# First batch entry: where the weight loads queue, how the coarse queries and keys are made, and unread products between the blocks

## The chip, the cores and the metric

One core of a Trainium2 chip runs the whole program. The time is that of the device in microseconds (us); three runs of the kernel before gave 1096.65, 1097.37 and 1098.7, median 1097.37.

## What is computed

Three layers follow each other. Attention takes 2 batch entries, 8 heads, 576 positions and 64 dimensions; each head is computed twice and added: once coarse, on means of four neighbouring positions, and once fine, where a position sees only positions less than 4 away.

```
q_d, k_d, v_d = means of 4 neighbouring positions of q, k, v        # 144 positions
out_d     = softmax(q_d k_d^T / 8) v_d,  each row repeated 4 times
out_local = softmax(q k^T / 8 where |i - j| < 4) v
x         = out_d + out_local                                       # 1152 x 512
```

Then come a mixture of 8 experts (512 to 1024 and back, weighted by a table P that 8 rounds of normalising rows and columns make) and an MLP (512 to 2048 and back). All inputs are float32.

## The kernel before, in words

Attention is done by units: a unit is a pair of heads of one batch entry. There are four units per entry, eight in all, and a unit is four blocks: the coarse block "c" and the fine blocks 0, 1, 2 of three tiles of 64 queries each. The loop over `stream` (from line 741) goes through the 32 blocks. For each it traces `scores` of this block, `turn` (the transpose of the softmax) of the block two back and `values` of the block three back. In the last two blocks of a unit it traces `setup` of the next unit, in three groups (g = 0, 1, 2), and in the last block `load` of the unit after that.

`load` (291) issues a unit's q, k and v on SyncE's queue. The q and k tile has one buffer, so the next load waits until `setup` has read it. `setup` (313) transposes three tiles of q and k on TensorE into a bank of PSUM (322). VectorE sums four neighbours from that bank (327) into `qkd`, and scales the queries out of it into `flat`, a tile whose other halves are zero (333). ScalarE and VectorE copy keys and queries for the fine blocks (337 to 339). GpSimd sums v (346, 347).

`scores` (349) multiplies: for the coarse block `flat` with `qkd` (355), for a fine block first the additive mask through an identity (362, bf16) and then queries with keys (368). VectorE takes the maximum (375), ScalarE the exponential (379), VectorE the division (380 to 382).

The weights of the experts are split into two parts of lower precision. `fetch_first` (113) loads one piece of the first weights by SyncE's queue into `raw` (two buffers), ScalarE rounds it (132, 138), VectorE and GpSimd make sums and remainders (133, 111, 139). `fetch_second` (141) does the same for the second weights (151 to 154). The first three pieces are traced in the attention loop, at line 747: one fetch in the second block of each of units 1 to 6.

From the third step after the middle of the stream on, `beside` (714) adds the first expert's products (601, 660) between the blocks of the second batch entry, a given number of columns for each block.

The order on each engine within attention is made by a planner: it plays the program through with its own costs and puts, on each engine, the instruction traced first among those that its play holds ready. After attention the order of TensorE is written out by hand. Each engine then runs its list strictly in that order.

Banks of PSUM: scores of the first batch entry take m0, m1 and m2 in turn (68); transposes take four banks called "at"; values take "y". In the second entry all of these take "at", and m0 to m2 belong to the expert's products (592).

Of the kernel before, what the change touches and what calls it, by code (L numbers as in the profile page):

```python
# [9 lines left out]
F32 = mybir.dt.float32  # L10
# [4 lines left out]
ALU = mybir.AluOpType  # L15
AX = mybir.AxisListType
# [4 lines left out]
def attention_moe_mlp(ctx: ExitStack, tc: tile.TileContext, q, k, v, w_gate, w1, w2, w_in, w_out, out):  # L21
    nc = tc.nc
    B, H, S, D = q.shape
    NT, DM = out.shape
    E, _, FF = w1.shape
    F2 = w_out.shape[0]
    P = 128
    R = 4
    SD = S // R
    HC = SD // 2  # L30
    QT = 64
    NQ = S // QT
    NB = 3
    CT = SD // NB
    KW = QT + 2 * R
# [15 lines left out]
    SUMS = 4  # L51
    OPS = 7

    const = ctx.enter_context(tc.tile_pool(name="const", bufs=1))
    xp = ctx.enter_context(tc.tile_pool(name="xp", bufs=1))
    wp = ctx.enter_context(tc.tile_pool(name="wp", bufs=3))
# [7 lines left out]

    def bank(tag, name):
        if tag == "m":
            tag = f"m{next(turns) % 3}"
        return ps.tile([P, 512], F32, tag=tag, bufs=4 if tag == "at" else 1, name=name)

    turns = count()  # L70
# [30 lines left out]
    s_out = scratch("s_out", [F2 // (2 * P), 2, P, 2, DM])  # L101

    weights = {}

    def weight_sums(sums, w):

# [168 lines left out]
    for x in fine + flat:  # L275
        nc.gpsimd.memset(x, 0.0)

    class Unit:


# [10 lines left out]
        def load(self, first=False):  # L291
            b, h0 = self.b, 2 * self.u
            self.qk = qk = ap.tile([P, NQ, 2, D], F32, tag="qk", bufs=1, name="qk")
            cuts = [slice(NB * g, NB * g + NB) for g in range(NB)] if first else [slice(0, NQ)]
            for cut in cuts:
                for w, src in enumerate((q, k)):
                    for hh in range(2):
                        nc.sync.dma_start(
                            qk[w * QT : (w + 1) * QT, cut, hh],
                            src[b, h0 + hh].rearrange("(t p) d -> p t d", p=QT)[:, cut],  # L300
                        )
            self.vw = vw = ap.tile([KW, NQ, 2, D], F32, tag="vw", name="vw")
            for t, w0 in ((0, 0), (NQ - 1, S - KW)):
                nc.sync.dma_start(vw[:, t], v[b, h0 : h0 + 2, w0 : w0 + KW, :].rearrange("h p d -> p h d"))
            for hh in range(2):
                src = v[b, h0 + hh, QT - R :, :]
                windows = bass.AP(tensor=src.tensor, offset=src.offset, ap=[[D, KW], [QT * D, NQ - 2], [1, D]])
                nc.sync.dma_start(vw[:, 1 : NQ - 1, hh], windows)
            self.vd = vd = ap.tile([HC, 2, 2, R, D], F32, tag="vd", bufs=1, name="vd")
            for hh in range(2):  # L310
                nc.sync.dma_start(vd[:, :, hh], v[b, h0 + hh].rearrange("(c p r) d -> p c r d", c=2, r=R))

        def setup(self, g):

            if g == 0:
                self.kT = ap.tile([P, NQ, QT], F32, tag="kT", name="kT")
                self.qkd = ap.tile([P, NQ, 2, QT // R], F32, tag="qkd", name="qkd")
            qkd = self.qkd
            tb = self.bank("tb", 1)
            tiles = slice(NB * g, NB * g + NB)  # L320
            for j in range(NB):
                nc.tensor.transpose(
                    tb[:, j * P : (j + 1) * P], self.qk[:, NB * g + j].rearrange("p h d -> p (h d)"), ident
                )
            tb = tb[:, : NB * P]
            tbv = tb.rearrange("x (t w p) -> x t w p", t=NB, w=2)
            nc.vector.tensor_reduce(
                qkd[:, tiles].rearrange("x t w g -> x (t w) g"),
                tb.rearrange("x (t g r) -> x t g r", g=QT // R, r=R), axis=AX.X, op=ALU.add,
            )  # L330
            for hh in range(2):
                half = slice(hh * D, (hh + 1) * D)
                nc.vector.tensor_scalar(
                    self.flat[half, g, hh].rearrange("x (j g) -> x j g", j=NB), qkd[half, tiles, 0],
                    SCALE / (R * R), None, op0=ALU.mult,
                )
            nc.scalar.mul(self.kT[:, tiles], tbv[:, :, 1], SCALE)
            nc.vector.tensor_copy(fine[g][:D, :, 0], tbv[:D, :, 0])
            nc.scalar.copy(fine[g][D:, :, 1], tbv[D:, :, 0])
            if g:  # L340
                return
            vd = self.vd

            self.vs = vs = ap.tile([HC, 2, 2, D], F32, tag="vs", name="vs")
            for c in range(2):
                nc.gpsimd.tensor_tensor(vd[:, c, :, 0:2, :], vd[:, c, :, 0:2, :], vd[:, c, :, 2:4, :], op=ALU.add)
                nc.gpsimd.tensor_tensor(vs[:, c], vd[:, c, :, 0, :], vd[:, c, :, 1, :], op=ALU.add)

        def scores(self, blk):

            sc = self.bank("sc", 0)
            if blk == "c":
                rows, w = 2 * CT, SD
                for i in range(NB):
                    nc.tensor.matmul(
                        sc[:rows, i * w : (i + 1) * w], self.flat[:, i].rearrange("x h q -> x (h q)"),
                        self.qkd[:, :, 1], start=True, stop=True,
                    )
            else:
                rows, w = P, KW  # L360
                tiles = range(NB * blk, NB * blk + NB)
                nc.tensor.matmul(
                    sc[:, : NB * w], identb, mask[:, blk : blk + NB].rearrange("p t w -> p (t w)"),
                    start=True, stop=False,
                )
                for i, t in enumerate(tiles):
                    w0 = min(max(t * QT - R, 0), S - KW)
                    nc.tensor.matmul(
                        sc[:, i * w : (i + 1) * w], fine[blk][:, i].rearrange("x h q -> x (h q)"),
                        self.kT.rearrange("x t q -> x (t q)")[:, w0 : w0 + KW], start=False, stop=(i == NB - 1),  # L370
                    )
# [369 lines left out]
    for n in range(len(stream) + LAG + 1):  # L741
        if n < len(stream):
            x, blk = stream[n]
            i, j = divmod(n, len(blocks))
            x.scores(blk)
            if j == 1 and 1 <= i <= 6:
                (fetch_first if i % 2 else fetch_second)((i - 1) // 2, (i - 1) // 2)
            if j >= 2 and i + 1 < len(units):
                for g in ((0, 1), (2,))[j - 2]:
                    units[i + 1].setup(g)  # L750
                if j == 3 and i + 2 < len(units):
                    units[i + 2].load()
        for lag, what in ((LAG, "turn"), (LAG + 1, "values")):
            if 0 <= n - lag < len(stream):
                x, blk = stream[n - lag]
                getattr(x, what)(blk)
        while columns < (n - begin) * DENSE:
            columns += next(side, 1 << 30)
# [100 lines left out]
```

## Time and profile before

| | |
|---|---|
| runs | 1096.65, 1097.37, 1098.7 us |
| profiled execution, first to last instruction (its span) | 1094.7 us |
| TensorE busy | 1060.0 us, 97% |
| VectorE busy | 727.0 us, 66% |
| ScalarE busy | 555.2 us, 51% |
| GpSimd busy | 537.6 us, 49% |

No other time of the profiled execution is shown than its span; the median of the runs is 2.67 us above it. A busy share is an average over the whole span; the first batch entry takes about the first 70 us of it. In the rows below, PE is TensorE, PEld its weight loads, DVE VectorE, ACT ScalarE, POOL GpSimd and SP SyncE. A number in brackets behind a timeline's row is the idle time of the engine just before, with what ended it. In a timeline several instructions of one kind are merged into one row with their count.

### The profile page before, as it was taken

What the parts mean: (1) busy time and instruction counts of PE and PEld (TensorE: products, weight loads), DVE (VectorE), ACT (ScalarE), POOL (GpSimd) and SP (SyncE); (2) the same over time, 40 slices, a digit from 0 to 9 for tenths busy, and PEclk for the clock granted to TensorE, in tenths of its full rate; (3) what the DMA queues carried; (4) which work ended last, traced back from release to release, by engine and by line L of the source; (5) the groups of instructions that cost most, each with busy time, mean ns of one, the idle gap of its engine ahead of it and who ended that gap; (6) DMA issues with size and microseconds to landing.
All of it is one profiled execution on the core that took longest, in us unless ns stands there. A gap on an engine that the chain in (4) does not pass through costs nothing.

```text
span 1094.7 us, 17873 instructions
## 1 busy us (share of the span) xinstructions
PE 1060.0 (97%) x6385; PEld 938.0 (86%) x6385; DVE 727.0 (66%) x1532; ACT 555.2 (51%) x1443; POOL 537.6 (49%) x569
## 2 busy tenths in 40 slices
PE   6899999999999999999999999999999998999998
PEld 5678888998987889888888988898898897889987
DVE  6889665565666676667657665766663578766765
ACT  4667645343444444434444443444443567676763
POOL 6735235464467676756766455354664212222321
PEclk9579999999999999999999999999999999999999
DMA  8454101111235334434443332223333273244112
GB/s 175 118 115 109 49 27 55 62 58 40 84 100 145 115 110 143 132 105 127 122 134 102 117 112 93 100 93 110 102 116 116 106 278 139 113 175 182 68 39 87
DMA packets 133497, 119.70 MB, mean 109 GB/s; under 512 B 35744, under 2 KB 111776, under 8 KB 133408
## 3 DMA queue, kind: packets, MB, share of 16 engines
q1 hardware_dynamic: 133408, 118.56, 35.0%
q8 instruction: 50, 0.82, 0.3%
q14 instruction: 39, 0.32, 0.1%
HBM read 93.11 MB, written 25.43 MB: 108 GB/s over the span
## 4 chain that ended last, share of the span: by engine, by line
PE 40%; POOL 5%; DMA 5%; DVE 3%; issue 2%; ACT 2%; SPq 0%; POOLq 0%; ACTq 0%; DVEq 0%
PE yps L660 21%; PE m L601 19%; DMA raw<-in_moe_w_out 2%; POOL sums L111 2%; POOL w2l L154 1%; POOL cva L188 1%; POOL cva L197 1%; DMA raw<-in_moe_w 1%; DMA raw<-in_moe_w_in 1%; DVE cva L178 1%; POOL w1l L139 1%; DVE cva L189 0%; DVE cva L179 0%; DVE cva L182 0%; DMA s_out<-cva 0%
## 5 line engine op out<-in xcount | busy, mean ns | idle before, releaser
L601 PE MATMUL m<-xh,w1h 128*128 128x320 f32 (+1 forms) x1120 | 336.6, 301 | 13.1 <-ACT t L610 6.3
L601 PE MATMUL m<-xh,w1l 128*128 128x320 f32 (+1 forms) x1120 | 332.5, 297 | 0.0
L601 PE MATMUL m<-xl,w1h 128*128 128x320 f32 (+1 forms) x1120 | 332.4, 297 | 0.0
L601 PEld LDWEIGHTS m<-xh,w1h 128*128 128x128 f32 x1120 | 212.2, 189 | 38.7 <-ACT t L610 10.8
L601 PEld LDWEIGHTS m<-xl,w1h 128*128 128x128 f32 x1120 | 212.4, 190 | 11.8
L601 PEld LDWEIGHTS m<-xh,w1l 128*128 128x128 f32 x1120 | 212.2, 190 | 0.2 <-issue 0.2
L660 PE MATMUL yps<-w2h,hh 128*128 128x512 f32 x502 | 198.5, 395 | 0.0
L660 PE MATMUL yps<-w2l,hh 128*128 128x512 f32 x502 | 198.4, 395 | 0.0
L660 PE MATMUL yps<-w2h,hl 128*128 128x512 f32 x502 | 195.5, 389 | 0.0
L660 PE MATMUL yps<-w2h,h 128*128 128x512 f32 x436 | 153.3, 393 | 0.0
L615 DVE TENSOR_TENSOR c<-m,t 128x256 f32<-128x256 f32 (+1 forms) x160 | 72.3, 452 | 100.9 <-PE m L601 99.5
L139 POOL TENSOR_TENSOR w1l<-sums,w1h 128x512 fp32r<-128x512 f32 x72 | 95.8, 1345 | 78.2 <-ACT w1h L138 54.4
L571 POOL TENSOR_TENSOR ab<-ab,up 128x320 f32<-128x320 f32 (+1 forms) x64 | 53.9, 843 | 157.2 <-ACT ln L567 109.8
L154 POOL TENSOR_TENSOR w2l<-raw,w2h 128x512 fp32r<-128x512 f32 x72 | 94.9, 1339 | 71.4 <-ACT w2h L153 71.3
L558 ACT ACTIVATE hh<-c 128x256 fp32r<-128x256 f32 (+1 forms) x138 | 60.0, 443 | 125.0 <-DVE c L615 123.3
L559 DVE SCALAR_TENSOR_TENSOR hl<-c,hh 128x256 fp32r<-128x256 f32 (+1 forms) x138 | 91.4, 668 | 35.0 <-ACT hh L558 33.2
L660 PEld LDWEIGHTS yps<-w2h,hl 128*128 128x128 f32 x502 | 94.4, 188 | 21.3
L677 DVE SCALAR_TENSOR_TENSOR acc<-yps,pr,acc 128x512 f32<-128x512 f32 x117 | 86.9, 743 | 29.5 <-PE yps L660 29.4
L660 PEld LDWEIGHTS yps<-w2h,hh 128*128 128x128 f32 x502 | 94.7, 189 | 12.6 <-DVE acc L673 0.2
L660 PEld LDWEIGHTS yps<-w2l,hh 128*128 128x128 f32 x502 | 94.7, 189 | 11.1 <-issue 0.4
L660 PEld LDWEIGHTS yps<-w2h,h 128*128 128x128 f32 x436 | 82.6, 189 | 14.8
L188 POOL TENSOR_TENSOR cva<-cva,raw 128x512 uint32<-128x512 uint32 x32 | 42.7, 1336 | 95.2 <-DVE raw L185 76.6
(134 smaller groups left out, 1700.7 us busy)
## 6 DMA issues: line engine op xcount, KB each, us to landing
raw<-in_moe_w SPq DMA_DIRECT2D x72, 256.0 KB
raw<-in_moe_w SPq DMA_DIRECT2D x36, 512.0 KB
w1h<-s_in SPq DMA_DIRECT2D x10, 896.0 KB
w1l<-s_in SPq DMA_DIRECT2D x10, 896.0 KB
raw<-in_moe_w_in SPq DMA_DIRECT2D x32, 256.0 KB
raw<-in_moe_w_out SPq DMA_DIRECT2D x16, 512.0 KB
w2l<-s_out SPq DMA_DIRECT2D x10, 512.0 KB
w2h<-s_out SPq DMA_DIRECT2D x10, 512.0 KB
```

Of the source, the lines that this page charges most:

```text
L111: nc.gpsimd.tensor_tensor(sums[i], a, b, op=op)
L139: nc.gpsimd.tensor_tensor(lo[:, part], sums, hi[:, part].bitcast(F32), op=ALU.subtract)
L154: nc.gpsimd.tensor_tensor(lo[:, i], raw[:, i], hi[:, i].bitcast(F32), op=ALU.subtract)
L178: nc.vector.tensor_scalar(a, high, 0x07FFFFFF, 3, op0=ALU.bitwise_and, op1=ALU.logical_shift_left)
L188: nc.gpsimd.tensor_tensor(a, a, low, op=ALU.add)
L558: nc.scalar.activation(hh, c, AF.Relu)
L559: nc.vector.scalar_tensor_tensor(out=hl, in0=c, scalar=0.0, in1=hh.bitcast(F32), op0=ALU.max, op1=ALU.subtract)
L571: nc.gpsimd.tensor_tensor(ab, ab, up, op=ALU.subtract)
L601: nc.tensor.matmul(b[:, :h], x[:, i, kk, :], y[s][:, i, kk, :], start=(not more and n == 0), stop=(n == 5), skip_group_check=more,)
L615: nc.vector.tensor_tensor(c, b[:, :h], t, op=ALU.add)
L660: nc.tensor.matmul(y, a[:, f, tok], b[:, f, :], start=(start and m == 0), stop=(stop and m == 5))
L677: nc.vector.scalar_tensor_tensor(out=acc[t], in0=y, scalar=pr[:, t, e : e + 1], in1=acc[t], op0=ALU.mult, op1=ALU.add,)
```

## The change

Four things change, all within attention.

1. The coarse queries and keys of the first batch entry come from TensorE. A small constant `coarse` holds, for each head of the pair, the matrix that adds four neighbours (queries scaled, the other head's columns zero). For each group of `setup`, six products of 48 columns with q and k as the weights go into a bank `pool` of the "at" kind; after the third group one copy by VectorE brings the bank into `parts`, from which the coarse scores read. The sums (327) and the scalings (333) are left out for these four units; the second entry keeps them.
2. Products of the mask with the identity, 360 columns in bf16, which nobody reads: 14 ahead of everything else, 3 after the scores of each block of the first entry. They are ordered behind the product traced before them; those between blocks have a lower priority.
3. These products write bank m2, so the scores of the first entry take m0 and m1 in turn.
4. The three pieces of weights that line 747 fetched one by one are traced with the loads of units 3, 4, 5 and 6, and their loads stand behind the last load of that unit on SyncE's queue.

```diff
+    START, BETWEEN, LOW = 14, 3, -60
-            tag = f"m{next(turns) % 3}"
+            tag = f"m{next(turns) % 2}"
+    BEHIND = {3: [(0, 0)], 4: [(0, 1), (1, 0)], 5: [(1, 1), (2, 0)], 6: [(2, 1)]}
+    group = ap.tile([P, 2, QT // R], F32, tag="qkd", name="group")
+    nc.vector.tensor_reduce(
+        group.rearrange("p w g -> p (w g)"), ident.rearrange("p (g r) -> p g r", r=R), axis=AX.X, op=ALU.add
+    )
+    coarse = ap.tile([P, 2, 3, QT // R], F32, bufs=1, name="coarse")
+    nc.vector.memset(coarse, 0.0)
+    for hh in range(2):
+        nc.vector.tensor_scalar(coarse[:, hh, hh], group[:, 0], SCALE / (R * R), None, op0=ALU.mult)
+        nc.vector.tensor_copy(coarse[:, hh, 2], group[:, 1])
+    warm = mask.rearrange("p t w -> p (t w)")
+    idle = ps.tile([P, 512], F32, tag="m2", name="idle")
+    def keep_warm(n):
+        for _ in range(n):
+            tc.keep_in_program_order(nc.tensor.matmul(idle[:, : (NB + 2) * KW], identb, warm, start=True, stop=True))
+    keep_warm(START)
...
+            if self.b == 0:
+                pool = self.pool[:, : NB * 3 * CT]
+                spread = pool.rearrange("x (i s j g) -> x i j s g", i=NB, s=3, j=NB)
+                for j in range(NB):
+                    for hh in range(2):
+                        nc.tensor.matmul(
+                            spread[hh * D : (hh + 1) * D, g, j], self.qk[:, NB * g + j, hh],
+                            coarse[:, hh].rearrange("p s g -> p (s g)"), start=True, stop=True,
+                        )
+                if g == NB - 1:
+                    self.parts = ap.tile([P, NB, 3 * CT], F32, tag="qkd", name="parts")
+                    nc.vector.tensor_copy(self.parts.rearrange("x i c -> x (i c)"), pool)
...
+            if self.b:
+                nc.vector.tensor_reduce(
...
+                    if self.b == 0:
+                        q_, k_ = self.parts[:, i, : 2 * CT], self.parts[:, :, 2 * CT :]
...
-            if j == 1 and 1 <= i <= 6:
-                (fetch_first if i % 2 else fetch_second)((i - 1) // 2, (i - 1) // 2)
+            if x.b == 0:
+                with tc.high_priority(offset=LOW):
+                    keep_warm(BETWEEN)
...
                     units[i + 2].load()
+                    with tc.issue_after(units[i + 2].loaded.ins):
+                        for f, second_part in BEHIND.get(i + 2, ()):
+                            (fetch_second if second_part else fetch_first)(f, f)
```

## Rows read from the trace of the kernel before

**Rows 1.** The page: busy time of TensorE over the span, and its clock by slices

```profile
PE 1060.0 (97%) x6385; PEld 938.0 (86%) x6385; DVE 727.0 (66%) x1532; ACT 555.2 (51%) x1443; POOL 537.6 (49%) x569
...
PEclk9579999999999999999999999999999999999999
```

**Rows 2.** The page: the chain that ended last, by engine

```profile
PE 40%; POOL 5%; DMA 5%; DVE 3%; issue 2%; ACT 2%; SPq 0%; POOLq 0%; ACTq 0%; DVEq 0%
```

**Rows 3.** Stretches: us long, busy of PE, PEld, DVE, ACT, POOL, clock, DMA share, GB/s

```profile
6.60:26.00 19.40, 16.50 (x78) 14.02 (x79) 16.26 (x42) 11.71 (x47) 10.95 (x16) 1.00 0.86 188
26.00:33.00 7.00, 4.72 (x61) 3.74 (x60) 6.83 (x18) 5.87 (x27) 7.00 (x10) 0.95 0.57 157
33.00:66.00 33.00, 29.71 (x174) 23.62 (x174) 28.79 (x75) 20.26 (x81) 21.13 (x25) 0.50 0.62 129
...
78.00:88.00 10.00, 9.33 (x63) 7.86 (x63) 8.88 (x30) 5.67 (x23) 2.56 (x4) 0.66 0.38 84
...
140.00:1094.70 954.70, 938.26 (x5461) 835.02 (x5459) 618.01 (x1220) 464.31 (x1088) 466.47 (x471) 1.00 0.33 108
```

**Rows 4.** Timeline of TensorE: start us, us, line, what, count

```profile
8.56 0.57 PE L362 MATMUL sc<-mask,identb 128*128 128x216 bf16 x2
...
14.45 1.54 PE L322 MATMUL tb<-ident,qk 128*128 128x128 f32 x6 [0.27 <-DMA qk<-in_k]
15.78 0.39 PE L362 MATMUL sc<-mask,identb 128*128 128x216 bf16 x1
...
27.41 0.57 PE L424 MATMUL pv<-et,vw 72*64 72x64 f32 x12
...
28.19 0.82 PE L322 MATMUL tb<-ident,qk 128*128 128x128 f32 x6
...
46.62 1.49 PE L322 MATMUL tb<-ident,qk 128*128 128x128 f32 x6
...
50.39 0.91 PE L424 MATMUL pv<-et,vw 72*64 72x64 f32 x12
...
66.70 0.36 PE L601 MATMUL m<-xh,w1h 128*128 128x256 f32 x1
```

**Rows 5.** VectorE by line and shape, 0 to 66 us: busy us, mean ns

```profile
L327 DVE TENSOR_REDUCE qkd<-tb 128x96 f32<-128x384 f32 x13 | 7.1, 549 | 6.2 <-PE tb L322 6.2
...
L333 DVE TENSOR_SCALAR flat<-qkd 64x48 f32<-64x48 f32 x24 | 4.6, 193 | 0.3
...
L375 DVE TENSOR_REDUCE small<-sc 96x3 f32<-96x432 f32 x4 | 2.4, 597 | 2.3 <-PE sc L355 2.3
```

**Rows 6.** VectorE by line and shape, 100 to 160 us: a plain copy

```profile
L671 DVE COPY acc<-yps 128x512 f32<-128x512 f32 x2 | 1.4, 689 | 0.0
```

**Rows 7.** Timeline of VectorE: the same product late and on time

```profile
33.54 3.70 DVE L382 TENSOR_TENSOR ex<-ex,small 128x216 f32<-128x216 f32 x1
...
39.53 0.37 DVE L382 TENSOR_TENSOR ex<-ex,small 128x216 f32<-128x216 f32 x1
```

**Rows 8.** Timeline of GpSimd: mask, first weight product, the one beside Rows 7

```profile
6.20 0.97 POOL L267 TENSOR_SCALAR_AFFINE_SELECT mask<-mask 64x216 bf16<-64x216 bf16 x3
...
26.62 2.64 POOL L139 TENSOR_TENSOR w1l<-sums,w1h 128x512 fp32r<-128x512 f32 x2
...
33.83 2.48 POOL L154 TENSOR_TENSOR w2l<-raw,w2h 128x512 fp32r<-128x512 f32 x2
```

**Rows 9.** Timeline of SyncE's queue: first weight load; last loads of units 3, 4

```profile
13.57 0.94 SPq L124 DMA_DIRECT2D raw<-in_moe_w  x2
...
38.14 0.59 SPq L311 DMA_DIRECT2D vd<-in_v  x1
...
61.70 0.77 SPq L311 DMA_DIRECT2D vd<-in_v  x2
```

**Rows 10.** Timeline of TensorE: its first products, and its wait at 33 us

```profile
6.61 2.15 PE L322 MATMUL tb<-ident,qk 128*128 128x128 f32 x9 [6.61 <-POOL mask L267]
...
33.34 1.18 PE L393 MATMUL tp<-ident,ex 96*72 96x96 f32 x6 [2.18 <-DVE ex L382]
```

More of the change, by code (lines that the diff above doesn't have):

```diff
@@ L310, in load @@
             for hh in range(2):
-                nc.sync.dma_start(vd[:, :, hh], v[b, h0 + hh].rearrange("(c p r) d -> p c r d", c=2, r=R))
+                self.loaded = nc.sync.dma_start(
+                    vd[:, :, hh], v[b, h0 + hh].rearrange("(c p r) d -> p c r d", c=2, r=R)
+                )
         def setup(self, g):
@@ L316, in setup @@
                 self.kT = ap.tile([P, NQ, QT], F32, tag="kT", name="kT")
-                self.qkd = ap.tile([P, NQ, 2, QT // R], F32, tag="qkd", name="qkd")
-            qkd = self.qkd
+                if self.b:
+                    self.qkd = ap.tile([P, 3 * NQ, QT // R], F32, tag="qkd", name="qkd")[:, : 2 * NQ]
+                    self.qkd = self.qkd.rearrange("x (t w) g -> x t w g", w=2)
+                if self.b == 0:
+                    self.pool = self.bank("pool", 1)
             tb = self.bank("tb", 1)
@@ L324, in setup @@
                 )
+            if self.b == 0:
[6 more added lines that the diff above has]
+                            coarse[:, hh].rearrange("p s g -> p (s g)"), start=True, stop=True,
+                        )
+                if g == NB - 1:
+                    self.parts = ap.tile([P, NB, 3 * CT], F32, tag="qkd", name="parts")
+                    nc.vector.tensor_copy(self.parts.rearrange("x i c -> x (i c)"), pool)
             tb = tb[:, : NB * P]
             tbv = tb.rearrange("x (t w p) -> x t w p", t=NB, w=2)
[L327 to L335, printed above, removed]
-                )
+            if self.b:
+                nc.vector.tensor_reduce(
+                    self.qkd[:, tiles].rearrange("x t w g -> x (t w) g"),
+                    tb.rearrange("x (t g r) -> x t g r", g=QT // R, r=R), axis=AX.X, op=ALU.add,
+                )
+                for hh in range(2):
+                    half = slice(hh * D, (hh + 1) * D)
+                    nc.vector.tensor_scalar(
+                        self.flat[half, g, hh].rearrange("x (j g) -> x j g", j=NB), self.qkd[half, tiles, 0],
+                        SCALE / (R * R), None, op0=ALU.mult,
+                    )
             nc.scalar.mul(self.kT[:, tiles], tbv[:, :, 1], SCALE)
@@ L354, in scores @@
                 for i in range(NB):
[L355 to L358, printed above, removed]
+                    if self.b == 0:
+                        q_, k_ = self.parts[:, i, : 2 * CT], self.parts[:, :, 2 * CT :]
+                    else:
+                        q_, k_ = self.flat[:, i].rearrange("x h q -> x (h q)"), self.qkd[:, :, 1]
+                    nc.tensor.matmul(sc[:rows, i * w : (i + 1) * w], q_, k_, start=True, stop=True)
             else:
```

## The prediction

> **What bounds the kernel now.** I read the page first. TensorE is busy for 1060.0 of 1094.7 us [rows 1], and in the chain that ended last it has by far the largest part that belongs to one engine [rows 2]. That is an average over stages, so I cut the span. From 140 us to the end TensorE is busy for 938.26 of 954.70 us [rows 3]: 16.4 us are idle there, the order of TensorE is written out by hand, and the change touches nothing of it. What the change can win lies ahead of 140 us, and there mostly in the first batch entry, up to about 66 us: at 66.70 the first product of the experts runs [rows 4]. A stage that ends earlier lets everything behind it start earlier, since TensorE is the bound of that rest.
>
> Within 6.6 to 66 us two engines are nearly full: TensorE is busy for 16.50 + 4.72 + 29.71 = 50.9 of 59.4 us and VectorE for 16.26 + 6.83 + 28.79 = 51.9 [rows 3]. The granted clock says 0.50 for 33 to 66 us, the lower level of 1.2 GHz, although TensorE was busy for 29.71 of those 33.00 us. The clock's row also says 1.00 for the first 26 us, and this the reader should not believe: six transposes of the same shape take 1.54 us at 14.45, 0.82 at 28.19 and 1.49 at 46.62 [rows 4]. The last stands in the stretch with 0.50, so the first ran at the lower level too, and the view does not show it. So 16.50 + 29.71 = 46.2 us of TensorE's work ran at the lower level. The full level costs 0.82/1.49 = 0.55 of that for the transposes and 0.57/0.91 = 0.63 for twelve products of the values [rows 4]; I take 0.59.
>
> **Part 1, coarse sums on TensorE.** Removed from VectorE, for four units of three groups: 12 sums of 0.549 and 24 scalings of 0.193 [rows 5], 6.6 + 4.6 = 11.2 us. Added there: four copies of 128x432 out of a bank. No row has that copy; a maximum over 432 columns takes 0.597 [rows 5], a copy of 512 columns 0.689 [rows 6]. I take 0.58 by columns from the second, 0.55 to 0.69 as ends: 2.3 us. The preparation of `coarse` is six small instructions in the first 6.6 us, where VectorE has next to nothing to do, so it costs nothing. VectorE's net is -8.9 us (ends -9.0 and -8.4). TensorE gets 18 products of 48 columns per unit, 72 in all. The nearest row is the product of the values with 64 columns: 0.57/12 = 0.048 us at the full level and 0.91/12 = 0.076 at the lower [rows 4], so 3.4 to 5.5 us. The coarse scores themselves keep their shape. The q and k buffer is released six short products later, 0.3 us at most per group, ahead of a load that is not late; cost 0.
>
> **Part 2, unread products.** A product of 216 bf16 columns takes 0.39 alone, two in a row 0.57 [rows 4], so each further one 0.18, at the lower level. For 360 columns that is 0.30, and 0.17 at the full level (by 0.55). The 48 between blocks are then 8.2 us at the full level and 14.4 at the lower. They are meant for idle time of TensorE; at the lower level there are only 59.4 - 50.9 = 8.5 us of it.
>
> The 14 at the start need the whole mask, which GpSimd ends at 6.20 + 0.97 = 7.17 [rows 8]. If they stand ahead of the first transposes, now at 6.61 [rows 10], they end at 7.17 + 14 x 0.30 = 11.4, and the transposes start 4.8 us late. If the planner puts them behind the transposes, the delay is less, down to 0. The price shrinks again: what stands between the first transposes and those of unit 1 (6.61 to 14.45, where a load is waited for) is 7.8 us at the lower level and 7.8 x 0.59 = 4.6 at the full one, so unit 1 would begin at 16.0 instead of 14.45. I take +1.6 us, ends 0 and +4.8.
>
> What is bought is the clock. If it stays at the full level, TensorE's work in the stage is 46.2 x 0.59 + 4.72 = 32.0, with the additions of both parts (3.4, 8.2, and 14 x 0.17 = 2.4) 46.0 us. VectorE's is 51.9 - 8.9 = 43.0.
>
> **Part 3, two banks for scores instead of three.** TensorE may run two blocks ahead of the softmax rather than three. There are 16 blocks in 59.4 us, 3.7 us each, and two banks allow 7.4 us from a bank's first product to its last exponential. No row shows a wait for such a bank. I take 0; the upper end is one short wait of 0.3 us in each block, 4.8 us.
>
> **Part 4, weight loads.** The first one now goes out at 13.57, ahead of the loads of unit 2, and its last remainder ends at 26.62 + 2.64 = 29.26 [rows 8, 9], 15.7 us later. In the change it stands behind unit 3's last load, now at 38.14 [rows 9], so it would be ready at 38.7 + 15.7 = 54.4, for a first use at 66.70. If loads come 5 us earlier and the first use 10, 7 us of slack are left. The next two stand behind unit 4's loads, now at 61.70 [rows 9]. The same instructions run on all engines, only later, so I take 0 for the work. What the early conversions did can be seen: a product of VectorE that takes 0.37 us at 39.53 took 3.70 at 33.54 [rows 7], while GpSimd made two remainders of the second weights from 33.83 to 36.31 [rows 8]. So the move clears units 0 to 2 of this and brings it to units 3 to 5. Ends: -3.3 (this one stall goes for good) and +3.3 (one more).
>
> A rule of the Trainium skill speaks against counting more here ("SBUF — State Buffer", section "Who interferes with whom"): a VectorE instruction with two operands from SBUF and a GpSimd one that reads SBUF exclude each other, and the later is blocked for the whole of the other. By it each remainder on GpSimd can block VectorE wherever it is put, so the move would win 0; by the one row at 33.54 alone it would win 3.3. The rows agree in part: the product is listed 0.29 us ahead of GpSimd's two remainders, yet it ended 0.93 us behind them.
>
> **The sum.** With the clock up, 46.0 us of TensorE and 43.0 of VectorE share a stage that today holds 51.9 of the fuller engine in 59.4, a fill of 0.87. At that fill VectorE's 43.0 need 49.4 us, and TensorE's 46.0 still fit in it (0.93, and 8.2 of them are filler). The stage is 10.0 us shorter; less 1.6 for the start is -8.4 us. The profiled execution's span is 1094.7; the median of the runs is 2.67 above it, and I let that stand: 1097.4 - 8.4 = 1089.0 us.
>
> **Rivals.**
>
> (a) More is won. With fewer waits VectorE fills 0.95 of the stage: 43.0/0.95 = 45.3, 14.1 less. And 78 to 88 us, where the clock fell to 0.66 on average with TensorE busy for 9.33 of 10.00 [rows 3], may stay at the full level: 0.68 of that stretch at the lower one costs 9.33 x 0.68 x 0.41 = 2.6. With the start that is -14.1 - 2.6 + 1.6 = -15.1, 1082 us. For it: VectorE reached 6.83 of 7.00 from 26 to 33 us [rows 3], just where TensorE was fast. Against it: that stretch was full of waits for GpSimd, and no unread products stand beyond the first entry.
>
> (b) The gain is eaten by SyncE's queue. `raw` has two buffers, a conversion takes 15.7 us, and now two fetches stand behind the loads of one unit. A weight load that waits for `raw` holds every later head load behind it. Unit loads 3 and 4 are 61.70 - 38.14 = 23.6 us apart today [rows 9]; at about 15 the second conversion is not over, and a hold of half a conversion, 8 us, brings 1097. Against it: the planner may put the head loads first.
>
> (c) Slower: the clock does not stay up, so the products do not do what they are there for. The row for it: TensorE was busy for nine tenths of 33 to 66 us, and the clock stayed at 0.50 [rows 3]; and it fell at 33 us when a transpose waited 2.18 us for VectorE [rows 10]. At the lower level throughout, TensorE has 46.2 + 4.72/0.59 + 5.5 + 14.4 + 4.2 = 78.3 us to do in a stage of 59.4: +18.9. Between that and 46.0 it reaches 59.4 when (59.4 - 46.0)/32.3 = 0.41 of the work is at the lower level; from there on the change loses. At two thirds it is 67.5, +8, 1105 us. Against it: the products are long and need no other engine, and the conversion that stalled VectorE at 33 us comes later.
>
> The Trainium skill ("TensorE: Matmul & The Clock Gate", section "Part 3: Packing small matmuls — row/col tiling") says that products start and end strictly in program order. By it an unread product behind a waiting one cannot fill that wait, and the 2.18 us ahead of 33.34 would stay empty; the trace agrees so far, nothing ran in them.
>
> **How the numbers follow.** My forecast 0.48, its own range 1084 to 1094; (a) 0.19; (b) 0.15; (c) 0.18. The range 1079 to 1101 holds nearly all of the forecast and of (b), most of (a) and the near edge of (c), a bit over 8 in 10. About 0.2%, 2.2 us, is what a measurement of this kernel tells from no change, so faster means under 1095.2: the forecast (nearly all), (a) and a quarter of (b), 0.70. Within is 0.11, mostly (b). Slower is (c) and a rest of (b), 0.19.
>
> **What would show it.** Six transposes near 0.82 us in every unit of the first entry, instead of about 1.5; VectorE without the 36 sums and scalings before 60 us and with four copies of 0.55 to 0.69; the first product of the experts at 56 to 60 us; from 140 us on the same idle time of TensorE, 16 us within 3. A clock at 0.50 over most of 15 to 55 us would make it wrong on the side of (c), a wait of SyncE's queue for `raw` with head loads behind it on that of (b), and a first transpose later than 11.4 us would break the price of the start.

## The result, and the profile after

The changed kernel takes 1109.99 us, the median of four runs (1108.88 to 1110.44), beside 1097.01 for the kernel before (1094.14 to 1098.7): 1.0132 times the time, 95% interval 1.0112 to 1.0152. I had forecast 1089.0 and a gain with 0.70. The profiled execution has a span of 1107.1 us, 12.4 more than before.

The page of the changed kernel, busy time of TensorE and its clock, as in [rows 1]:

```profile
PE 1067.0 (96%) x6591; PEld 938.9 (85%) x6591; DVE 719.8 (65%) x1506; ACT 557.1 (50%) x1443; POOL 538.6 (49%) x569
...
PEclk9888999999999999999999999999999999999999
```

VectorE is busy for 7.2 us less and TensorE for 7.0 more. The same stretches as in [rows 3], with the same columns:

```profile
6.60:26.00 19.40, 18.34 (x157) 13.04 (x158) 8.00 (x22) 8.28 (x38) 6.56 (x13) 1.00 0.48 102
26.00:33.00 7.00, 7.00 (x75) 5.64 (x74) 4.88 (x18) 5.16 (x24) 1.57 (x4) 1.00 0.78 188
33.00:66.00 33.00, 25.58 (x267) 18.90 (x268) 24.62 (x55) 22.52 (x83) 20.87 (x24) 0.83 0.61 141
78.00:88.00 10.00, 7.72 (x85) 6.53 (x84) 8.59 (x27) 7.68 (x31) 6.59 (x8) 1.00 0.87 195
140.00:1107.10 967.10, 947.21 (x5521) 842.43 (x5519) 621.72 (x1228) 468.53 (x1105) 473.73 (x476) 1.00 0.33 108
```

The last row splits the loss. At 140 us TensorE still has 947.21 us of work before it, 8.95 more than before; and of the time from there on it idles 967.10 - 947.21 = 19.9 us, 3.4 more than the 16.4 of before. That is the 12.4 us. The clock did come up (0.83 instead of 0.50 from 33 to 66), and VectorE is idle for more than half of the first 19.40 us (8.00 busy, before 16.26). The loss begins behind that: TensorE is idle for 7.4 us from 33 to 66 (before 3.3), and for 2.3 us from 78 to 88 (before 0.7). The timeline of TensorE, answering to [rows 4, 10]:

```profile
6.57 0.87 PE L351 MATMUL tb<-ident,qk 128*128 128x128 f32 x3 [6.57 <-DMA qk<-in_k]
...
9.83 4.18 PE L298 MATMUL idle<-mask,identb 128*128 128x360 bf16 x14
...
14.19 0.55 PE L351 MATMUL tb<-ident,qk 128*128 128x128 f32 x3
...
38.03 0.69 PE L436 MATMUL tp<-ident,ex 96*72 96x96 f32 x3 [2.31 <-ACT fine L381]
...
39.88 0.90 PE L351 MATMUL tb<-ident,qk 128*128 128x128 f32 x3 [0.22 <-ACT etc L440]
...
59.75 0.57 PE L467 MATMUL pv<-et,vw 72*64 72x64 f32 x12 [0.80 <-ACT xc L463]
63.82 0.85 PE L445 MATMUL tp<-ident,ex 128*72 128x128 f32 x3 [3.50 <-DVE ex L425]
...
65.80 1.54 PE L351 MATMUL tb<-ident,qk 128*128 128x128 f32 x6
...
72.81 0.39 PE L644 MATMUL m<-xh,w1h 128*128 128x256 f32 x1
```

Three transposes take 0.55 at 14.19, the full level. The first long wait is one for ScalarE: it ends at 38.03, after 2.31 us, and three transposes behind it take 0.90, the lower level. ScalarE was late because a rounding of the moved weights stood in its list and waited 1.80 us, until 36.79, for its load. At 63.82 TensorE has waited 3.50 us for a division of VectorE, and behind it six transposes take 1.54, the lower level again. The experts' first product comes at 72.81, 6.1 us later than in [rows 4]. What VectorE did ahead of that division:

```profile
56.02 0.95 DVE L137 TENSOR_TENSOR w1l<-raw,w1h 128x256 fp32r<-128x256 f32 x1
56.89 0.94 DVE L246 TENSOR_TENSOR xl<-xf,xh 128x256 fp32r<-128x256 f32 x1
...
58.62 1.35 DVE L137 TENSOR_TENSOR w1l<-raw,w1h 128x512 fp32r<-128x512 f32 x1
...
60.41 1.65 DVE L246 TENSOR_TENSOR xl<-xf,xh 128x256 fp32r<-128x256 f32 x1
...
62.41 0.39 DVE L246 TENSOR_TENSOR xl<-xf,xh 128x256 fp32r<-128x256 f32 x1
...
63.01 0.76 DVE L425 TENSOR_TENSOR ex<-ex,small 128x216 f32<-128x216 f32 x1
```

and GpSimd beside it:

```profile
53.03 2.79 POOL L158 TENSOR_TENSOR w2l<-raw,w2h 128x512 fp32r<-128x512 f32 x2 [0.66 <-ACT w2h L157]
55.77 1.78 POOL L115 TENSOR_TENSOR sums<-raw 128x256 f32<-128x256 f32 x2
57.51 0.90 POOL L115 TENSOR_TENSOR sums<-raw,sums 128x256 f32<-128x256 f32 x1
58.38 1.05 POOL L389 TENSOR_TENSOR vs<-vd 72x128 f32<-72x128 f32 x2
59.39 1.17 POOL L115 TENSOR_TENSOR sums<-raw,sums 128x256 f32<-128x256 f32 x1
60.52 1.26 POOL L143 TENSOR_TENSOR w1l<-sums,w1h 128x512 fp32r<-128x512 f32 x1
```

The reader should put the two side by side. GpSimd has no gap from 53.03 to 61.78. In that time the same `xl` of 256 columns takes VectorE 0.94 and 1.65 us that takes it 0.39 at 62.41, when GpSimd pauses. This is what [rows 7, 8] showed at 33.54, now in front of a division that TensorE waits for. The sum of such lost time did not grow. The same division, as a mean over 6.6 to 100 us, before and after:

```profile
L382 DVE TENSOR_TENSOR ex<-ex,small 128x216 f32<-128x216 f32 x16 | 10.6, 669 | 0.1
```

```profile
L425 DVE TENSOR_TENSOR ex<-ex,small 128x216 f32<-128x216 f32 x15 | 8.5, 569 | 0.2
```

It is stretched less in the changed kernel (alone it takes about 0.37 us), so what matters is where a stretched instruction falls, not how many there are.

### The profile page after: what moved, and what is told of

It is laid out like the page before. It is cut to its first block, busy times and chain, and to the rows that moved or that the text cites. A ratio compares the mean times of both kernels' runs of the same rounds, so it can differ in the third digit from the quotient of the medians.

```text
span 1107.1 us, 18248 instructions
## 1 busy us (share of the span) xinstructions
PE 1067.0 (96%) x6591; PEld 938.9 (85%) x6591; DVE 719.8 (65%) x1506; ACT 557.1 (50%) x1443; POOL 538.6 (49%) x569
## 4 chain that ended last, share of the span: by engine, by line
PE 33%; POOL 7%; DMA 6%; DVE 5%; issue 3%; ACT 2%; SPq 0%; POOLq 0%; DVEq 0%; ACTq 0%
PE yps L703 18%; PE m L644 16%; POOL sums L115 3%; DMA raw<-in_moe_w_out 2%; DMA raw<-in_moe_w 2%; POOL w2l L158 1%; POOL cva L192 1%; POOL cva L201 1%; DMA raw<-in_moe_w_in 1%; DVE cva L182 1%; DVE cva L193 1%; DVE cva L183 1%; POOL w1l L143 1%; DVE cva L186 1%; DMA s_in<-cva 0%
## 5 line engine op out<-in xcount | busy, mean ns | idle before, releaser
L644 PEld LDWEIGHTS m<-xh,w1h 128*128 128x128 f32 x1120 | 212.6, 190 | 41.8 <-ACT t L653 12.4
L703 PEld LDWEIGHTS yps<-w2h,hl 128*128 128x128 f32 x502 | 94.5, 188 | 21.5
L703 PEld LDWEIGHTS yps<-w2l,hh 128*128 128x128 f32 x502 | 95.0, 189 | 10.7
```

What stands on the lines that cost most here:

```text
L644: nc.tensor.matmul(b[:, :h], x[:, i, kk, :], y[s][:, i, kk, :], start=(not more and n == 0), stop=(n == 5), skip_group_check=more,)
L703: nc.tensor.matmul(y, a[:, f, tok], b[:, f, :], start=(start and m == 0), stop=(stop and m == 5))
```

## Experiments

### Which part costs the time

Part 4 alone (`l_only`), and everything but Part 4 (`c_w`: the fetches back at their old place). The edit of `c_w`:

```diff
+            if j == 1 and 1 <= i <= 6:
+                (fetch_first if i % 2 else fetch_second)((i - 1) // 2, (i - 1) // 2)
...
-                    with tc.issue_after(units[i + 2].loaded.ins):
-                        for f, second_part in BEHIND.get(i + 2, ()):
-                            (fetch_second if second_part else fetch_first)(f, f)
```

> Only part 4: the weight loads stand behind the head loads; coarse sums, three banks and no unread products as before. Theory A (the moved weights cost: their conversions stand in the lists of ScalarE and VectorE ahead of softmax work and wait there for loads that have not landed, and GpSimd's remainders now meet units 2 to 4): 6 to 13 us slower than before, first product of the experts after 70 us. Theory B (the unread products and the lost third bank cost): within 3 us of before, or faster. Theory C (any edit reshuffles the planner's lists and the total moves by chance): no sign foreseen, and the parts will not add up.

> Parts 1 to 3 without part 4: coarse sums on TensorE, unread products, two banks; the weights are fetched where they were. Theory A: faster than before by 5 to 10 us, since VectorE has 9 us less to do and the clock is up; first product before 62 us. Theory B: 8 to 13 us slower, as the whole change. Theory C: anything within 12 us either way.

Measured: Part 4 alone 1107.58, ratio 1.0098 (1.0071 to 1.0124); parts 1 to 3 together 1093.38, ratio 0.9972 (0.9948 to 0.9996), a version that beats both kernels, the one before only just, and by less than the 5 to 10 us that I expected. So Part 4 costs 10.7 us alone and 1109.99 - 1093.38 = 16.6 on top of the rest, and parts 1 to 3 win 3.5 where I had 8.4. Then parts 1 to 3 taken apart, and Part 4 with Part 1:

```diff
 # part 1 alone: no unread products, three banks, fetches as before
-    keep_warm(START)
...
-                    keep_warm(BETWEEN)
...
 # parts 2 and 3 alone: sums and scalings on VectorE as before
-            if self.b:
+            if True:
                 nc.vector.tensor_reduce(
...
-            if self.b == 0:
+            if False:
                 pool = self.pool[:, : NB * 3 * CT]
```

> Only part 1: coarse queries and keys by TensorE, three banks for scores, no unread products, loads as before. Theory A and B alike: VectorE is relieved of 9 us, but TensorE stays at the lower clock and gets 5.5 us more, so 0 to 5 us faster. Theory C: anything within 12 us either way.

> Only parts 2 and 3: unread products (14 and 3 per block) and two banks for scores; coarse sums by VectorE, loads as before. Theory A: the clock is up for most of the first entry, 2 to 6 us faster. Theory B: the products and the missing bank hold up TensorE, 5 to 13 us slower. Theory C: anything within 12 us either way.

> Parts 1 and 4: coarse sums on TensorE and the loads held back, but no unread products and three banks. Theory A: as slow as the whole change or slower (the clock is not helped either), 1107 to 1118. Theory B: near the kernel before, 1094 to 1100.

Measured: Part 1 alone 1102.55, ratio 1.0051 (1.0027 to 1.0075); parts 2 and 3 alone 1106.13, 1.0075 (1.0057 to 1.0094); parts 1 and 4 1110.06, 1.0124 (1.0098 to 1.015), as slow as the whole change. Each half of parts 1 to 3 loses by itself, 5.7 and 9.3 us, and together they win: their prices do not add, and for Part 1 alone I had expected a gain of 0 to 5. So theory C of the expectations, that an edit reshuffles the planner's lists and moves the total by chance, is not excluded for parts 1 to 3. Against it for Part 4 speaks that it costs 7.5, 10.7 and 16.6 us in three surroundings (on Part 1, alone, on parts 1 to 3), always with the same sign.

### What Part 4 costs: the conversions beside VectorE, or the hold?

Three versions of the whole change. Without the hold, so that the planner is free to load earlier; with ScalarE's roundings later; and without GpSimd's share of the conversions (its sums and remainders of the first three pieces). The edits:

```diff
 # a_noqueue
-                    with tc.issue_after(units[i + 2].loaded.ins):
...
 # a_later: convert_first/convert_second run in the next unit's second block
+            if j == 1:
+                with tc.issue_after(x.exp.ins):
+                    while kept:
+                        kept.pop(0)()
...
 # a_nopool, in fetch_first (and likewise in fetch_second)
+        if f < 3:
+            nc.gpsimd.memset(lo[:, :SUMS].bitcast(F32), 0.0)
+            for i in range(2):
+                nc.scalar.copy(hi[:, 2 * i : 2 * i + 2], raw[:, :, :, i, :])
+            return
```

> The whole change, but its weight loads are not held behind the head loads: they are traced at the same places, and the planner is free to queue them earlier. Theory A (holding the loads back is what costs): 1088 to 1099, the loads go out early as before. Theory B (unread products or the missing bank): still near 1110. Theory C (chance of the lists): not told.

> The whole change, with the roundings of the first three pieces put later on ScalarE: behind the exponential of block 0 of the next unit, so that their loads have landed when their turn comes. Theory A2 (lists wait for loads): the 1.8 and 2.0 us waits of ScalarE for the raw weights at 32 to 37 us go, 3 to 6 us faster than the whole change, 1104 to 1107 or less. Theory A1: no better than 1108, since GpSimd's remainders only move later. Theory B: near 1110.

> The whole change, but the first three pieces of weights leave out GpSimd's part: no sums and no remainders of these pieces are computed, GpSimd sets the remainders to zero early, and ScalarE rounds the raw weights instead of the sums (so these outputs are not the reference's). Loads and ScalarE's work stay. Theory A1 (GpSimd's conversions, now beside units 2 to 4, block VectorE): 1090 to 1100. Theory A2 (ScalarE's and VectorE's lists wait for the loads themselves): stays at 1105 to 1112. Theory B: near 1110.

Measured: 1102.07 (1.0048, 1.0032 to 1.0064) without the hold, where the first weight load goes out at 8.85 instead of 29.80, 7.9 us less than the whole change and in the range of neither theory; 1109.85 (1.0112, 1.0089 to 1.0134) with the roundings later; 1099.09 (1.0036, 1.0018 to 1.0054) without GpSimd's share, 10.9 us less than the whole change. The longest waits of TensorE from 6.6 to 70 us behind its first load, in all, count and longest, in the whole change:

```profile
PE tp L445 <- DVE ex L425: 3.5, 1, 3.5
PE tp L436 <- ACT fine L381: 2.3, 1, 2.3
PE sc L405 <- ACT ex L422: 1.0, 1, 1.0
PE pv L467 <- ACT xc L463: 0.8, 1, 0.8
```

and without GpSimd's share:

```profile
PE tb L360 <- ACT ex L431: 1.1, 1, 1.1
PE tp L454 <- DVE qkd L378: 0.6, 1, 0.6
```

The roundings did hold ScalarE up, but putting them later only moved the collision. In that version the wait of 2.31 us is gone and the experts' first product comes at 63.64, earlier than in either kernel. Then a remainder on VectorE meets a run of GpSimd without a gap from 60.94 to 67.61:

```profile
63.62 2.87 DVE L143 TENSOR_TENSOR w1l<-raw,w1h 128x256 fp32r<-128x256 f32 x1
```

and TensorE waits for a sum behind it in VectorE's list:

```profile
70.34 0.74 PE L468 MATMUL pv<-etc,vs 72*64 72x144 f32 x2 [4.47 <-DVE xf L494]
```

That execution is the slowest of the version's four (1115.06).

But a kernel with less to do may be faster anyway. So the same was left out of the other versions:

> The kernel before without GpSimd's sums and remainders of the first three pieces of the weights (they are set to zero; ScalarE's roundings and VectorE's remainders stay): the base for the next three. Lock-out theory (a VectorE instruction that reads SBUF waits until GpSimd's run of instructions has a gap): VectorE's lost time of 4 to 6 us in each window up to 66 us goes, of which the stall of 3.70 at 33.54 is on the path: 1090 to 1094. Rival (the lost time lies under other waits, TensorE at the lower level is what bounds): 1095 to 1098.

> Part 4 alone, without GpSimd's sums and remainders of the first three pieces. Part 4 alone cost 10.7 us with them. Lock-out theory: that price is GpSimd's, so this stands within 3 us of the kernel before with the same left out. Rival (the roundings on ScalarE and the remainders on VectorE, now in units 2 to 4, and the later weights themselves cost the time): 7 to 11 us above it.

> Parts 1 to 3 with the weight loads where they were before, without GpSimd's sums and remainders of the first three pieces. The whole change with the same left out gave 1099.1, and parts 1 to 3 with them 1093.4. Lock-out theory, whole: this comes within 3 us of 1099.1 or below it by what the early run of GpSimd still costs, at most 5: 1094 to 1099 would say that holding the loads back has no other price. Rival (holding them back also costs by itself, by VectorE's own pieces and ScalarE's roundings in units 2 to 4): 1085 to 1091.

> Parts 2 and 3 alone, without GpSimd's sums and remainders of the first three pieces. With them these parts cost 9.3 us, and their trace has a VectorE product of 5.80 us (0.38 by itself) under a run of GpSimd, with TensorE waiting 5.28 us for it and the granted clock at 0.50 behind it. Lock-out theory: without that run the stall goes, and the parts come out within 3 us of the kernel before with the same left out, or faster by up to 6 as the clock stays up. Rival (the unread products or the missing bank cost the time themselves): 6 to 10 us above it.

Measured, with the work that TensorE has left at 140 us and its idle time behind that (span less 140 less the work), both from the one profiled execution, which need not be a typical run (the runs of one version lie up to 15 us apart; the one of Part 4 alone is the slowest of 6 at 1113.24, its counterpart without the share at 1094.41 is 5.8 below its median, and the one of parts 1 to 3 is the fastest of 12 at 1087.87):

| version | with GpSimd's share: median, work left, idle | without it: median, work left, idle |
|---|---|---|
| before | 1096.87, 938.26, 16.4 | 1096.80, 936.47, 20.2 |
| part 4 alone | 1107.58, 952.37, 19.1 | 1100.19, 932.54, 20.1 |
| parts 1 to 3 | 1093.38, 928.70, 17.4 | 1096.14, 934.68, 21.5 |
| parts 2, 3 | 1106.13, 944.42, 19.8 | 1101.77, 941.82, 21.7 |
| whole change | 1109.99, 947.21, 19.9 | 1099.09, 936.48, 20.3 |

The ratios without the share are 1.0013 (1.0001 to 1.0024), 1.0029 (1.0012 to 1.0047), 0.9989 (0.997 to 1.0009) and 1.0029 (1.0003 to 1.0056). The kernel before wins nothing by it: there the collisions cost nothing that can be measured, and my expectation of 1090 to 1094 was a miss. Without the share, parts 2 and 3 stay 5.0 above the kernel before, where I had at most 3. Part 4's price falls from 10.7 to 3.4 us alone, and from 16.6 to 3.0 on top of parts 1 to 3 (by the ratios to about 2 and 5). So most of the price is that of GpSimd's share, though these runs take out its collisions with VectorE and ScalarE's waits for its sums together; that it is the collisions is read from the timelines. The work left at 140 us goes the same way: Part 4 alone had 14.1 us more to do than the kernel before, and has 3.9 less; the whole change had 18.5 more than parts 1 to 3, and has 1.8 more. These differences overstate it, since the executions behind them lie at the ends of their versions' runs; the medians are the measure. The two rows of Part 4 alone, with and without GpSimd's share (us long, busy of TensorE, clock, DMA share, GB/s):

```profile
140.00:2000.00 1860.00, 952.37 (x5570) 1.00 0.17 56
```

```profile
140.00:2000.00 1860.00, 932.54 (x5378) 1.00 0.17 56
```

How hard a collision can be shows in Part 4 alone, on VectorE:

```profile
49.55 4.52 DVE L469 COPY rest<-xf 128x64 f32<-128x64 f32 x1
```

on GpSimd:

```profile
49.22 1.14 POOL L369 TENSOR_TENSOR vs<-vd 72x128 f32<-72x128 f32 x2 [2.02 <-PE pv L436]
50.32 1.26 POOL L143 TENSOR_TENSOR w1l<-sums,w1h 128x512 fp32r<-128x512 f32 x1
51.54 2.48 POOL L158 TENSOR_TENSOR w2l<-raw,w2h 128x512 fp32r<-128x512 f32 x2
55.90 1.32 POOL L143 TENSOR_TENSOR w1l<-sums,w1h 128x512 fp32r<-128x512 f32 x1 [1.88 <-ACT w1h L142]
```

and on TensorE:

```profile
55.19 1.28 PE L381 MATMUL sc<-qkd,flat 128*96 128x144 f32 x4 [5.07 <-DVE qkd L349]
```

A copy of 64 columns is listed with 4.52 us, until GpSimd's run ends at 54.0, and TensorE waits 5.07 for the sum behind it. With parts 2 and 3 alone a division that takes 0.38 by itself met a run of GpSimd without a gap from 17.60 to 28.77:

```profile
21.16 5.80 DVE L415 TENSOR_TENSOR ex<-ex,small 128x216 f32<-128x216 f32 x1
```

```profile
27.11 0.82 PE L435 MATMUL tp<-ident,ex 128*72 128x128 f32 x3 [5.28 <-DVE ex L415]
```

TensorE waited 5.28 us for it, and from 26 to 33 us the granted clock was 0.50. Last, the loads one unit earlier:

```diff
-    BEHIND = {3: [(0, 0)], 4: [(0, 1), (1, 0)], 5: [(1, 1), (2, 0)], 6: [(2, 1)]}
+    BEHIND = {2: [(0, 0)], 3: [(0, 1)], 4: [(1, 0)], 5: [(1, 1)], 6: [(2, 0), (2, 1)]}
```

> The whole change with the weight loads queued one unit earlier (the first behind unit 2's loads, the last two behind unit 6's). Lock-out theory: the conversions then fall into units 1 to 3, where VectorE is nearer to its slack of the start, and Part 4's price of 16.6 us shrinks to between a third and two thirds: 1098 to 1105. Rival (any conversion behind the head loads costs the same; the hold itself is the price): 1107 to 1111.

Measured: 1105.63, ratio 1.0072 (1.0044 to 1.01), between the two ends: about a quarter of the 16.6 us is gone, just less than the third that the lock-out theory wanted.

### What parts 1 to 3 win, and why not more

```diff
 # cw_b1, cw_b5, on parts 1 to 3
-    START, BETWEEN, LOW = 14, 3, -60
+    START, BETWEEN, LOW = 14, 1, -60      # cw_b5: 14, 5, -60
...
 # cw_b0 (cs3 as well, with three banks)
-                    keep_warm(BETWEEN)
...
-            tag = f"m{next(turns) % 2}"   # cs3
+            tag = f"m{next(turns) % 3}"   # cs3
...
 # cw_s0
-    keep_warm(START)
```

> Parts 1 to 3 with one unread product between blocks instead of three. In the trace with three, a group of three takes 0.62 us behind other products and one more product 0.15, and TensorE is busy for 32.11 of 33.00 us from 33 to 66. Theory F (the unread products fill TensorE, which is now the bound): 32 products of 0.15 fewer, up to 4.8 us less: 1088 to 1091, and the clock stays up. Theory K (they earn their time by the clock): the clock falls in parts of 30 to 66 us and the time rises towards that of part 1 alone, 1096 to 1102.

> Parts 1 to 3 without the products between blocks; the 14 at the start and the two banks stay. Theory F: 48 products fewer, 7.2 us less than 1093.4 at best, 1086 to 1091. Theory K: 1096 to 1102, with 0.50 granted in some of the stretches from 26 to 66 us.

> As the one before it, with three banks for scores as in the kernel before. By the prediction the bank costs nothing: within 2 us of that run. If the missing bank takes the gain of parts 1 to 3: 3 to 6 us below it, and the waits of score products for an exponential (1.6 us in 12 blocks with two banks) are gone.

> Parts 1 to 3 without the 14 products at the start; three between blocks stay. They take 3.37 us, between the second and the third group of unit 0's transposes. If they earn their time by the clock: transposes of units 0 and 1 stay near 0.9 for three instead of 0.55, the clock comes up a unit later, and the time is 1096 to 1101. If the time they take is the dearer: 1089 to 1092.

> Parts 1 to 3 with five unread products between blocks instead of three: 32 more of 0.15 us, 4.8 us of TensorE, in a stretch in which it is busy for 32.11 of 33.00 us and the clock is at the lower level for a few us only. Theory F past the best number: 1096 to 1099. If the runs with three often lose the clock (their times spread from 1087.9 to 1102.2) and five hold it: 1088 to 1092, with a smaller spread.

Measured on top of parts 1 to 3, with the mean granted clock of a whole run, median over the runs:

| products at the start, between blocks | us | ratio, interval | clock |
|---|---|---|---|
| 14, none, two banks | 1103.70 | 1.0063 (1.0044 to 1.0082) | 0.982 |
| 14, none, three banks | 1103.37 | 1.0054 (1.0036 to 1.0073) | 0.982 |
| 14, one | 1096.47 | 0.9998 (0.9983 to 1.0013) | 0.989 |
| 14, three | 1093.38 | 0.9972 (0.9948 to 0.9996) | 0.996 |
| 14, five | 1100.26 | 1.0032 (1.0016 to 1.0049) | 0.996 |
| none, three | 1100.75 | 1.0029 (1.0006 to 1.0052) | 0.991 |

From none to three products the clock rises and the time falls by 10.3 us. Three is the best number tried by the median, with one 3.1 us behind and intervals that overlap; five hold the same clock and cost 6.9 us more. The third bank is worth nothing (tried without products between blocks). Without the 14 at the start the time is 7.4 us worse. The stretches of parts 1 to 3 (TensorE only: us long, busy, clock, DMA share, GB/s) without products between blocks:

```profile
26.00:33.00 7.00, 6.34 (x35) 0.50 0.42 104
33.00:66.00 33.00, 31.95 (x295) 0.72 0.61 126
```

with three, by all engines as in [rows 3]; the last row is the stretch up to the first product of the experts:

```profile
26.00:33.00 7.00, 5.92 (x32) 3.96 (x32) 5.24 (x11) 5.30 (x19) 5.17 (x6) 0.76 0.75 158
33.00:66.00 33.00, 32.11 (x373) 25.46 (x373) 28.11 (x83) 25.25 (x112) 19.96 (x25) 1.00 0.57 122
...
6.60:65.23 58.63, 53.31 (x540) 39.92 (x540) 44.29 (x111) 39.76 (x160) 39.61 (x50) 0.97 0.68 155
```

With three, TensorE is the bound: 53.31 of 58.63 us, 32.11 of 33.00 in the middle, at the full level. Without them it is as full, at the lower level for longer. That the products earn their time by the clock rests on these two things together, the clock that rises and TensorE that is full at either level.

The stage itself did not get shorter by it, even in this fastest of twelve runs. The transposes of the first unit of the second entry mark its end; they began at 63.40 in the kernel before, and here:

```profile
63.48 0.82 PE L351 MATMUL tb<-ident,qk 128*128 128x128 f32 x6
```

The 9.6 us less that TensorE has left at 140 us show mostly behind this point, where among other things the clock stays at 1.00 (before 0.66 from 78 to 88); the rest was not taken apart. The opposite happens in the whole change without GpSimd's share:

```profile
54.98 0.85 PE L360 MATMUL tb<-ident,qk 128*128 128x128 f32 x6 [1.07 <-ACT ex L431]
```

There the stage is 8.4 us shorter, as I had forecast for the change, and at 140 us only 1.8 us of it are left (936.48 against 938.26).

The scatter of the runs agrees. The twelve runs of Part 1 alone go from 1092.97 at a mean clock of 0.998 to 1107.61 at 0.981, and clock and time are correlated with -0.86; with parts 1 to 3 it is -0.86 as well. In 119 runs of the kernel before it is -0.12: the 34 runs with a clock of 0.9935 and more have a median of 1096.46, the 45 under 0.982 one of 1096.74. The kernel before is as fast with the clock down as with the clock up. A correlation does not say which is the cause: a run in which TensorE waits longer can also have the lower clock for it.

## Why the prediction was wrong, by its steps

The forecast was -8.4 us, measured was +13.0, 21.4 apart. Part 4, taken at 0, cost 16.6 on top of the rest; parts 1 to 3, taken at -8.4, gave -3.5.

**Part 4 failed first.** The step is "the same instructions run on all engines, only later, so I take 0 for the work", with ends of 3.3 to either side. The work is the same, but its price depends on what stands beside it. In the kernel before, GpSimd's share begins at 19.65 us and costs nothing that can be measured (1096.80 without it). After the change VectorE is idle for 11.4 of the first 19.40 us, and the share begins at 36.90 and runs beside VectorE's operands for the experts. I had the mechanism before me in [rows 7, 8] and wrote that the move brings it to units 3 to 5; I priced one stall, not a run of GpSimd beside which VectorE's operand pieces take twice as long or more for 9 us, and not the fall of the clock behind the waits of 2.31 and 3.50 us. Nor did I price ScalarE's roundings, which waited for the held loads. The rule I set against it ("SBUF — State Buffer", "Who interferes with whom", in the Trainium skill) says that the later one is blocked for the whole of the other instruction and so left the move at 0. The trace agrees that they exclude each other, and shows more than the rule as I put it: a one-operand copy of VectorE held through three GpSimd rows, 4.52 us. My own row says so too: GpSimd ran on behind the two remainders of [rows 8] until 37.00 us, and the product listed at 33.54 ended at 37.24, with that run.

**The sum of parts 1 to 3 failed on two terms, both TensorE's.** TensorE was to need 46.0 us and needed 53.31. The old work was right: 46.2 x 0.59 + 4.72 = 32.0 forecast, and 53.31 less the two rows below is 31.6. The additions were not. TensorE by line and shape in parts 1 to 3, from 6.6 to 65.2 us:

```profile
L298 PE MATMUL idle<-mask,identb 128*128 128x360 bf16 x62 | 13.2, 343 | 0.0
...
L359 PE MATMUL pool<-coarse,qk 128*64 128x48 f32 x144 | 8.5, 241 | 0.0
```

The coarse sums are 144 listed instructions, not 72: a float32 product is listed twice, so the twelve of [rows 4] that I divided 0.57 by were six products, and 3.4 us became 8.5. The miscount makes 6.8 of that; the rest is at least in part the lower level, at which the first twelve rows took 0.89 instead of 0.56. The unread products took 13.2 instead of 10.6; the 14 at the start ran partly at the lower level, 3.37 us (4.18 in the whole change). VectorE's term was right (43.0 forecast, 44.29 measured). But the stage was sized by VectorE's fill of 0.87, and with TensorE at 53.31 of 58.63 it could not shrink to 49.4, and did not. "A stage that ends earlier lets everything behind it start earlier" failed too, where a stage did end 8.4 us earlier: 1.8 us of it were left at 140. So the 3.5 us that parts 1 to 3 won did not come by the sum that I had made: the clock did come up as forecast, but that the sign came out right for these parts is partly luck.

**What the clock buys was right only for the changed kernel.** By the 119 runs a lower mean clock costs the kernel before nothing measurable. Once VectorE is relieved, TensorE is the bound, and the times follow the level.

**Small terms.** The four copies took 0.595 us each (forecast 0.58). The start cost the first transposes nothing: they began at 6.57, and the 14 ran between the second and third group. But the q and k buffer, taken at 0, did come free late, and the load of unit 1 with it:

```profile
15.26 1.30 SPq L322 DMA_DIRECT2D qk<-in_q  x2
```

That load went out at 8.79 in the kernel before, at 12.85 with Part 1 alone and at 14.55 with parts 1 to 3, and unit 1's first transposes began at 21.01 instead of 14.45, where I had 16.0. Six coarse products took 0.89 us at the start, not 0.3, and the 14 stand ahead of the third group. What this delay costs at the end no run separates. The two banks cost 0 where they were tried. SyncE's queue, rival (b), did hold a weight load for 9.8 us behind `raw`, but only at 104.88, and TensorE waited for no load from 7 to 140 us. Rival (c) had the right sign and the wrong reason: the clock was up until TensorE waited for ScalarE (2.31 us) and VectorE (3.50 us).

**Behind 140 us** I had expected the same idle time within 3 us. It is 16.4 before and 19.9 after. In all 19 other kernels it is 17.4 to 21.7, though none edits the code of that part, each from one execution. Why the kernel before has the least was not tried and stays open, and so does why Part 1, and parts 2 and 3, lose alone. The slow runs of Part 1 are those with a low clock, but the kernel before has clocks as low at no cost, and parts 1 to 3 have the late load of unit 1 as well and win. For parts 2 and 3 the one stall at 21.16 accounts for part of 9.3 us (4.4 us are gone without GpSimd's share). Part 4's price without GpSimd's share, about 3 us, and the 8.7 us that the version without the hold stays above parts 1 to 3 have no run of their own.

## What to carry to other kernels

Moved work costs what its new neighbours make it cost: before taking 0 for a move, look at the busy share of every engine in the stretch that it leaves and in the one that it enters, and read how long the neighbours' instructions take while it runs, and which of them another engine waits for. A stage's own length is no measure of the gain: read the work that the bounding engine has left at a fixed time further on. Filler for the clock paid here only together with the relief of VectorE, and it must be summed as work of that engine; the number is found by trying (here none, one, three, five: 1103.7, 1096.5, 1093.4, 1100.3). The scatter of a kernel's own runs, clock against time, gives a hint whether the clock bounds it, before anything is changed.

## What the runs showed of the hardware

An uninterrupted run of GpSimd instructions can hold one VectorE instruction for many times its own length, even a copy with one operand: 4.52 us for 64 columns (another copy of that form took 0.18), 5.80 for a division of 0.38. Milder, it doubles them: 0.94 instead of 0.39 for 256 columns. And mean granted clocks between 0.975 and 1.000 went with the same time of one kernel over 119 runs, while in another, with one part changed, a spread from 0.975 to 0.998 went with times up to 14.6 us apart.
